# A transformer block forward and backward: one 256 KB load per head in place of four, and fewer DMAs on ScalarE's queue in the backward attention loop

## The chip, the cores and the metric

One core of one Trainium2 chip runs the whole program in one launch. The metric is the device time of an execution in microseconds (us). The engines are PE (matmuls; PEld is its weight load), DVE (VectorE), ACT (ScalarE), POOL (GpSimd) and SP (SyncE, which here only issues DMAs). ACT and POOL can issue DMAs too; an issue stands in the engine's own instruction queue.

## The reference

A block with adaptive layer norm, computed forward and then differentiated. The sequence has S = 2048 tokens of D = 512, 32 heads of 16, and a feed-forward part of width 1792. All arrays are bf16.

```python
mod = silu(c) @ w_mod            # sa, ca, ga, sb, cb, gb: six rows of 512
h = layernorm(x) * (1 + ca) + sa
q, k, v = split(h @ wqkv)        # 32 heads of 16
p = softmax(q @ k.T * 16 ** -0.5)
x = x + ga * ((p @ v) @ wo)
h = layernorm(x) * (1 + cb) + sb
x = x + gb * (relu(h @ w1 + b1) ** 2 @ w2 + b2)
# returned: x, and the gradients of sum(x * grad_out) with respect to
# x, wqkv, wo, w1, b1, w2, b2, c, w_mod
```

## The kernel before

The program has three stretches. The **forward stretch** (to about 1040 us) makes the projections, runs attention by chunks of 512 queries and, a chunk behind, the feed-forward part with its backward pass. It leaves in DRAM what the backward attention needs, feature-major (one row of 2048 tokens for each of the 512 features): `qkT_st` (k and q), `vT_st`, `dOT_st`, and for each head one row of softmax offsets `m_st` and one of sums `d_st`; token-major it leaves `q_st`, `k_st`, `dOs_st`. The **last chunk** (`last_chunk`, to about 1125 us) finishes the dense part and fetches the first head group's rows meanwhile (`head_loads`). The **backward attention loop** (1125 to 2380 us) follows, and then a **tail** with the projections' gradients.

The backward loop treats 8 groups of 4 heads. A head has 16 features, so its rows occupy 16 of 32 partitions, and partition 16 of each 32 holds its `m` or `d` row. The tiles of a group are `k`, `v`, `q`, `do` (128 partitions x 2048 tokens each, profile names `ik`, `iv`, `iq`, `ido`) and `qs` (`iqs`, the group's q token-major). There are two such sets, `hsets[0]` and `hsets[1]`; group hg uses the set hg % 2, and the set of the next group is filled during this one.

A group has 64 units (4 blocks of keys x 16 tiles of queries), four units to a block, so 16 blocks. The order of the instructions on PE, ACT, DVE, SP and POOL is written out by hand: `order_t` and `order_n` are lists of tokens, one list per block in turn, which is why two blocks form the period of the loop. Per unit and head, `score` (L1603) makes a score tile of 128 x 512 on PE, `expo` (L1609) its exponential on ACT; per pair of heads, `dp_pair` (L1623, L1625) makes dP on PE and multiplies by the exponential on DVE into `dS_u`. `k_quad` (L1663) and `v_quad` (L1672) accumulate the gradients of k and v in PSUM (`accVK`).

The gradient of q needs `dS` transposed. `transpose_unit` has SP do this with DMA transposes into `dsT`: two units in one (L1640), and in every second block the third unit alone (L1638); the fourth unit of such a block is transposed on PE (`pe_turn`) and copied by ACT (L1769). Two blocks later `dq_quad` (L1690, `dqacc`) uses `dsT`, and `dq_out` moves the result over ACT (`dqtmp`) and POOL into `dQacc` and `dQst`.

The DMAs beside the transposes are issued on ACT's queue: `at(j, load, to, fro)` puts one behind step j of the loop, where a step is one `D` token (half a unit; 128 to a group), and `load` (L1585) is `ACT.dma_start`. `plan_head(hg)` sets the loads of group hg at every fourth step from step 14 of the group before:

```python
            j0 = (hg - 1) * 128 + 14
            loads = list(kvq_loads(hg)) + list(row_loads(hsets[hg % 2]["do"], dOT_st, hg, slice(0, n), d_st))
            for i, (to, fro) in enumerate(loads):
                at(j0 + 4 * i, load, to, fro)
            at(j0 + 40, spread_qz, hg)
```

`kvq_loads` gives 4 loads of `qs`, then 4 of k, 4 of q with one for the `m` rows, and 4 of v; `row_loads` for dO gives 4 and one for the `d` rows: 22 in all, of 64 KB each but the two for `m` and `d` (16 KB). `spread_qz` copies `qs` into a zero-padded tile on POOL. Each of the four key blocks ends with a store of `vkb` to `dVKtP` (128 KB, groups 0 to 5), and the group with four stores of `dQst` to `dQc` (64 KB each, groups 0 to 6), both on ACT's queue too.

Of the kernel before, what the change touches and what calls it, by code (L numbers as in the profile page):

```python
# [20 lines left out]
P = 128  # L21
# [13 lines left out]
def kernel(  # L35
# [52 lines left out]
    q_st = dram.tile([HG, P, TT, 64], BF, name="q_st")  # L88
    k_st = dram.tile([P, TT, D], BF, name="k_st")
    v_st = dram.tile([n, D], BF, name="v_st")  # L90
    qkT_st = dram.tile([2, D, n], BF, name="qkT_st")
    vT_st = dram.tile([D, n], BF, name="vT_st")
    dOT_st = dram.tile([D, n], BF, name="dOT_st")
    m_st = dram.tile([H, n], BF, name="m_st")
    d_st = dram.tile([H, n], BF, name="d_st")
    wpad_st = dram.tile([D, 8 * P], BF, name="wpad_st")
    wT_st = dram.tile([12, P, D], BF, name="wT_st")
    wmT_st = dram.tile([6, P, 4, D], BF, name="wmT_st")
# [48 lines left out]
    with ExitStack() as ph:  # L147
# [398 lines left out]
        def fload(qc, hg):  # L546
            i = hg % 2
            kt_sb, qt_sb = kts[i], qts[i]
            rows = list(row_loads(kt_sb, qkT_st[1], hg, slice(0, n)))
            rows += row_loads(qt_sb, qkT_st[0], hg, slice(512 * qc, 512 * qc + 512), m_st)  # L550
# [207 lines left out]
        qkT_v = qkT_st.rearrange("a (b p) n -> p a b n", p=P)  # L758
        psp = {}

        def wmod_slice(j):
# [5 lines left out]
        def chunk_cols(g):  # L767
            return slice(512 * g, 512 * g + 512)
# [84 lines left out]
        def prep():  # L853
# [84 lines left out]
            for g in range(QC):  # L938
# [26 lines left out]
                if g == 2:  # L965
                    square(sq[:, 4, :], sP[:, 4, :])
                    norms(4)
            sp(qkT_st[1, 0:P, :], KTs[0][:])
            sp(qkT_st[0, 0:P, 0:512], sP[:, 4, :])
            widest(2)  # L970
            square(sq[:, 3, :], KTs[0][:, chunk_cols(3)])
            norms(3)
# [23 lines left out]
        def plan_tasks():  # L996
# [5 lines left out]
            def key_tile(b, g):  # L1002
                if g == 0:
                    KTs[b] = cb.tile([P, n], BF, name="KT", tag=xtags[b])
                if "k" not in T:
                    T["k"] = cb.tile([P, 4, D], BF, name="sqK", tag="a_c")
                acc = mm()
                turned_proj(acc[:], 1, g, b)
                DVE.tensor_copy(KTs[b][:, chunk_cols(g)], acc[:])
                square(T["k"][:, g, :], KTs[b][:, chunk_cols(g)])  # L1010
                if g == QC - 1:
                    later(1, sp, qkT_st[1, b * P:(b + 1) * P, :], KTs[b][:])

            def key_norm(b, g):
                pn = mm()
# [3 lines left out]
            def query_tile(g, hb):  # L1019
                if "q" not in T:  # L1020
                    T["q"] = cb.tile([P, 4, D], BF, name="sqQ", tag="xn2_c")
                lo = 4 + 4 * (g % 2)
                acc = mm()
                turned_proj(acc[:], 0, g, hb)
                DVE.tensor_copy(sP[:, lo + hb, :], acc[:])
                square(T["q"][:, hb, :], sP[:, lo + hb, :])
                if g == 0:
                    later(1, sp, qkT_st[0, hb * P:(hb + 1) * P, 0:512], sP[:, lo + hb, :])
                elif hb == 3:
                    later(1, sp, qkT_v[:, 0, :, chunk_cols(g)], sP[:, lo:lo + 4, :])  # L1030

            def query_norm(hbs):
                pn = mm()
# [168 lines left out]

        def head_set(i):
            strm.append(tc.alloc_tile_pool(name=f"phIs{i}", bufs=1, side="right"))
            hs = {key: strm[i].tile([P, n], BF, name=f"i{key}{i}") for key in ("k", "v", "q", "do")}
            hs["qs"] = strm[i].tile([P, TT, 64], BF, name=f"iqs{i}")
            hsets.append(hs)

        def head_fill(i):
            for key in ("k", "v", "q", "do"):  # L1210
                POOL.memset(hsets[i][key][:], 1.0 if key in ("k", "v") else 0.0)

        def kvq_loads(hg):
            hs = hsets[hg % 2]
            for i in range(4):
                yield hs["qs"][:, 4 * i:4 * i + 4, :], q_st[hg][:, 4 * i:4 * i + 4, :]
            yield from row_loads(hs["k"], qkT_st[1], hg, slice(0, n))
            yield from row_loads(hs["q"], qkT_st[0], hg, slice(0, n), m_st)
            yield from row_loads(hs["v"], vT_st, hg, slice(0, n))

        def spread_qz(hg):
            to, fro = qz[hg % 2][:, :, :, DH:2 * DH], hsets[hg % 2]["qs"].rearrange("p t (h d) -> p t h d", h=4)
# [19 lines left out]
        def last_chunk(O_c, L, w1T, w2T):  # L1242
# [76 lines left out]
            later(17, copy_const, hsets[0]["v"][:], 1.0)  # L1319
# [182 lines left out]
        with ExitStack() as ph2:  # L1502
            pools["mm"] = ph2.enter_context(tc.tile_pool(name="psM2", bufs=4, space=bass.MemoryType.PSUM))
            with tc.manual_schedule(engines={PE.engine, ACT.engine, DVE.engine, SP.engine, POOL.engine}):
                pools["rs"] = pools["mm"].tile([P, 512], F32, name="rsums", tag="rs", bufs=1)
                DVE.memset(pools["rs"][:], 0.0)
                unit[0] += 1
                run_due()
                L = loads["L"]
                L_dw.append(ffw.tile([P, FC * D], BF, name="dwbuf", tag="wB"))  # L1510
                vaugpool.release()
                head_set(0)
                DVE.memset(hsets[0]["q"][:], 0.0)
                DVE.memset(hsets[0]["do"][:], 0.0)
                copy_const(hsets[0]["k"][:], 1.0)
                O_c = late_finish()
                sp(L["gfT"].rearrange("p t o q -> p (t o) q"), flat(L["gf"]), True)
                for i in range(4):
                    fetch_part(i)
                att.close()  # L1520
                qzpool = tc.alloc_tile_pool(name="qzpool", bufs=1, side="right")
                qz = [qzpool.tile([P, TT, 4, 32], BF, name="qz0")]
                kpool = tc.alloc_tile_pool(name="kpool", bufs=1, side="right")
                dpool = tc.alloc_tile_pool(name="dpool", bufs=1, side="right")
                dwr = tc.alloc_tile_pool(name="dwr", bufs=1, side="right")
                w2T = kpool.tile([P, DC, FF], BF, name="w2T_1", tag="ks")
                for s in range(4):
                    sp(w2T[:, s, :], w2T_st[:, s, :])
                w1T = dpool.tile([P, FC, D], BF, name="w1T_1", tag="dt")
                for s in range(7):  # L1530
                    sp(w1T[:, 2 * s:2 * s + 2, :], w1T_st[:, 2 * s:2 * s + 2, :])

                def head_loads():
                    done = slice(0, 512 * (QC - 1))
                    for i, (to, fro) in enumerate(list(kvq_loads(0)) + list(row_loads(hsets[0]["do"][:, done], dOT_st, 0, done, d_st))):
                        later(i, sp, to, fro)
                    later(12, copy_const, qz[0].rearrange("p t h d -> p (t h d)"), 0.0)
                    later(16, spread_qz, 0)

# [17 lines left out]
    with ExitStack() as ph:  # L1557
# [108 lines left out]
        def v_quad(u):  # L1666
# [57 lines left out]
        for hg in range(1, HG):  # L1724
            plan_head(hg)
        for i, key in enumerate(("q", "k", "v", "do")):
            at((HG - 1) * 128 + 14 + 8 * i, load_grads, "vk", i, hsets[0][key][:])
# [50 lines left out]
    with ExitStack() as ph:  # L1778
# [6 lines left out]
        xs["dq", 1], xs["dq", 2], xs["vk", 4], xs["vk", 5] = (hsets[1][key] for key in ("q", "k", "v", "do"))  # L1785
        xs["dq", 3] = qz[1].rearrange("p t h d -> p (t h d)")
        for key, dsrc, i in (("dq", dQc, 1), ("vk", dVKtP, 4), ("dq", dQc, 2), ("vk", dVKtP, 5)):
            SP.dma_start(out=xs[key, i][:], in_=dsrc[i])
# [271 lines left out]
```

## Time and profile before

| | us |
|---|---|
| runs: median, lowest, highest of 3 | 2517.32, 2511.94, 2524.12 |
| profiled execution, first to last instruction | 2517.6 |
| backward loop within it | 1125 to 2380 |
| one transpose of two units on SP's queue (L1640), median | 5.36 |
| one exponential of 128 x 512 (L1609), from start to start | 0.48 |
| issue of one load on ACT's queue (L1585), median | 0.31 to 0.33 |

The trace's times are of this one profiled execution and count from its first instruction. A row such as `2100.50 0.32 ACTq L1585 DMA_DIRECT2D ik<-qkT_st` gives start, duration, engine, line of the kernel, operation and tiles; `ACTq` and `SPq` are the queues of ACT and SP, where DMA issues stand. Brackets at the end of a row give the engine's idle time ahead of it and what ended it. ACT's exponentials overlap, so a start-to-start distance says more than a duration. A row of windows has the stretch, its length, busy time and count of each engine, the granted TensorE clock (1.00 is full), the share of the DMA engines and GB/s.

### The profile page before, as it was taken

How to read it: one execution, taken by the hardware profiler on the slowest of the kernel's cores; microseconds unless marked ns; L12 is line 12 of the kernel's file. 1: busy time of each engine (PE TensorE's matmuls, PEld its weight loads, DVE VectorE, ACT ScalarE, POOL GpSimd, SP SyncE). 2: the span in 40 equal slices, each digit the busy share in tenths (PEclk: the TensorE clock that was granted, in tenths of full speed). 3: DMA queues.
4: the chain of work that ended last, by engine and by line, in shares of the span. 5: the costliest groups of instructions: out<-in, count | busy, mean ns of one | idle time of the engine just before them, and what ended most of it. 6: DMA issues, size and time to landing. Idle time of an engine off the chain costs nothing. (4 is left out here: it accounts for less than half of the span.)

```text
span 2517.6 us, 49897 instructions
## 1 busy us (share of the span) xinstructions
PE 2342.5 (93%) x19005; PEld 776.3 (31%) x19005; DVE 1810.1 (72%) x2341; ACT 2302.3 (91%) x3577; POOL 350.0 (14%) x379
## 2 busy tenths in 40 slices
PE   7899889989988999999999999999999999999999
PEld 3232223222322323442233322233323323322343
DVE  5556153454435454579999999999999999998862
ACT  7999999999989999539999999999999999999842
POOL 2000000211323142210111101111010111100100
PEclk9999999999999999999999999999999999998999
DMA  6476455367658766979999999999999999999972
GB/s 202 136 193 165 150 122 139 96 161 144 103 85 176 151 134 119 261 208 191 202 199 210 196 206 208 201 207 202 207 202 202 209 195 203 195 208 212 196 237 72
DMA packets 1220981, 447.15 MB, mean 178 GB/s; under 512 B 1096951, under 2 KB 1191607, under 8 KB 1220486
## 3 DMA queue, kind: packets, MB, share of 16 engines
q1 hardware_dynamic: 1192822, 409.11, 82.2%
q0 software_dynamic: 10944, 16.78, 4.8%
q10 hardware_dynamic: 16976, 18.07, 2.8%
q8 instruction: 149, 2.44, 0.4%
q14 instruction: 90, 0.74, 0.1%
HBM read 96.75 MB, written 73.95 MB: 68 GB/s over the span
## 5 line engine op out<-in xcount | busy, mean ns | idle before, releaser
L1625 DVE TENSOR_TENSOR dS_u<-psD_u,E_u 128x1024 bf16<-128x1024 f32 x1024 | 1186.0, 1218 | 71.6 <-PE psD_u L1623 24.0
L567 ACT ACTIVATE ET<-psST 128x1024 bf16<-128x1024 f32 x1024 | 942.0, 1260 | 27.0 <-PE psST L565 26.5
L1609 ACT ACTIVATE E_u<-psS_A 128x512 bf16<-128x512 f32 x768 | 513.1, 668 | 10.5 <-PE psS_C L1603 8.5
L1609 ACT ACTIVATE E_u<-psS_B 128x512 bf16<-128x512 f32 x768 | 505.8, 659 | 12.1 <-DMA dsT<-dS_u 3.0
L1623 PE MATMUL psD_u<-iv,ido 32*128 32x512 bf16 x2048 | 409.6, 388 | 0.0
L565 PE MATMUL psST<-qt_sb,kt_sb 32*128 32x512 bf16 x2048 | 317.8, 387 | 62.0 <-ACT ET L567 46.6
L1609 ACT ACTIVATE E_u<-psS_C 128x512 bf16<-128x512 f32 x512 | 335.4, 655 | 3.3 <-PE psS_B L1603 1.4
L1603 PE MATMUL psS_B<-ik,iq 32*128 32x512 bf16 x768 | 295.3, 385 | 12.8 <-ACT E_u L1609 5.5
L1603 PE MATMUL psS_A<-ik,iq 32*128 32x512 bf16 x768 | 293.4, 382 | 10.9 <-DVE dwlast L237 1.0
L1603 PEld LDWEIGHTS <-iq 32*128 32x128 bf16 x2048 | 130.2, 91 | 316.1 <-issue 298.8
L1663 PE MATMUL accVK<-dS_u,qz 128*32 128x512 bf16 x2048 | 213.3, 390 | 0.4 <-PE psD_u L1623 0.2
L581 PE MATMUL oacc<-ET,vaug 128*32 128x512 bf16 x2048 | 207.7, 396 | 2.2 <-DVE ostage L585 2.2
L1672 PE MATMUL accVK<-E_u,dOs_tok 128*16 128x512 bf16 x2048 | 204.1, 387 | 0.0
L1708 POOL TENSOR_TENSOR dQacc<-dQacc,dqtmp 128x512 f32<-128x512 f32 x64 | 81.2, 1268 | 852.0 <-ACT dqtmp L1703 852.0
L1603 PE MATMUL psS_C<-ik,iq 32*128 32x512 bf16 x512 | 194.7, 380 | 4.2
L565 PEld LDWEIGHTS <-kt_sb 32*128 32x128 bf16 x2048 | 85.8, 91 | 352.2 <-issue 324.6
L1690 PE MATMUL dqacc<-dsT,KS_tok 128*32 128x512 bf16 x2048 | 146.5, 384 | 18.5 <-DMA dsT<-dS_u 4.3
L1769 ACT ACTIVATE dsT<-ptT 128x1024 bf16<-128x1024 bf16 x128 | 145.8, 1139 | 7.9 <-PE ptT L1653 7.3
L251 DVE COPY part<-pm 128x512 f32<-128x512 f32 (+2 forms) x103 | 63.5, 617 | 114.8 <-PE pm L233 111.5
L1623 PEld LDWEIGHTS <-ido 32*128 32x128 bf16 x2048 | 104.6, 91 | 98.9 <-issue 92.9
L1663 PEld LDWEIGHTS <-qz 128*32 128x32 bf16 x2048 | 58.4, 94 | 177.9 <-issue 162.9
L581 PEld LDWEIGHTS <-vaug 128*32 128x32 bf16 x2048 | 53.1, 93 | 121.4 <-issue 121.4
(407 smaller groups left out, 2516.3 us busy)
## 6 DMA issues: line engine op xcount, KB each, us to landing
p_st<-part POOLq DMA_DIRECT2D x36, 256.0 KB, 5.2
kt_sb<-qkT_st SPq DMA_DIRECT2D x124, 64.0 KB
wA<-in_B_w_dram SPq DMA_DIRECT2D x28, 256.0 KB
wB<-w1T_st SPq DMA_DIRECT2D x21, 256.0 KB
wA<-w2T_st SPq DMA_DIRECT2D x21, 256.0 KB
wB<-in_B_w_dram SPq DMA_DIRECT2D x21, 256.0 KB
p_st<-part POOLq DMA_DIRECT2D x25, 192.0 KB, 5.3
p_st<-part SPq DMA_DIRECT2D x18, 256.0 KB
```

The costliest lines, as they stand in the source:

```text
L565: PE.matmul(ps[:, hi, :], kt_sb[r:r + 32, kt * P:(kt + 1) * P], qt_sb[r:r + 32, :], start=True, stop=True, tile_position=(r, 0))
L567: ACT.activation(ET[:, 2 * pair:2 * pair + 2, :], ps[:], AF.Exp, scale=SCALE)
L581: PE.matmul(oacc[32 * hq:32 * hq + 32, :], lhsT, ET[:, hq, :], start=(kt == 0), stop=(kt == TT - 1), tile_position=(0, 32 * hq), skip_grou ...
L1603: PE.matmul(psS[:], st["q"][r:r + 32, qt * P:(qt + 1) * P], st["k"][r:r + 32, kc * 512:kc * 512 + 512], start=True, stop=True, tile_positi ...
L1609: ACT.activation(bst[u][0][:, hq, :], sst.pop((u, hq))[:], AF.Exp, scale=SCALE)
L1623: PE.matmul(psD[:, hi, :], st["do"][r:r + 32, qt * P:(qt + 1) * P], st["v"][r:r + 32, kc * 512:kc * 512 + 512], start=True, stop=True, til ...
L1625: DVE.tensor_tensor(dS_u[:, 2 * pair:2 * pair + 2, :], psD[:], E_u[:, 2 * pair:2 * pair + 2, :], ALU.mult)
L1663: PE.matmul(cur["vk"][32 * hq:32 * hq + 32, :], hst[hg]["qz"][:, qt, hq, :], bst[u][1][:, hq, :], start=(qt == 0), stop=False, tile_positi ...
L1672: PE.matmul(acc[32 * hq:32 * hq + DH, :], dOs_tok[:, qt, (hg * 4 + hq) * DH:(hg * 4 + hq + 1) * DH], E_u[:, hq, :], start=False, stop=(qt ...
L1690: PE.matmul(acc[32 * hq:32 * hq + 32, :], KS_tok[:, kc * 4 + kt, h * DH:h * DH + 32], tT[:, :, hq * 4 + kt, :], start=(kt == 0), stop=(kt ...
L1708: POOL.tensor_tensor(dst2, dst, tmp[:], ALU.add)
L1769: ACT.activation(dst, pt[:], AF.Identity)
```

## The change

The four feature-major arrays become one DRAM tile in which the k, v, q and dO rows of a feature stand side by side, and so do the four tiles of a set in SBUF. One load then brings all four rows of a head's 16 features (16 rows of 16 KB), and one load of 8 KB runs the `m` and `d` rows of the four heads; `qs` comes in one load instead of four. A group has 6 loads, at every 13th step. The stores of `vkb` go two key blocks at a time. In the last chunk the first group's k, v and q come with four loads of 12 KB rows, and dO by itself as before. The places that wrote or read the old arrays use slices of the new ones.

```diff
-    qkT_st = dram.tile([2, D, n], BF, name="qkT_st")
-    vT_st = dram.tile([D, n], BF, name="vT_st")
-    dOT_st = dram.tile([D, n], BF, name="dOT_st")
-    m_st = dram.tile([H, n], BF, name="m_st")
-    d_st = dram.tile([H, n], BF, name="d_st")
+    rows4_st = dram.tile([D, 4, n], BF, name="rows4_st")
+    kT_st, vT_st, qT_st, dOT_st = (rows4_st[:, i, :] for i in range(4))
+    md_st = dram.tile([H, 2, n], BF, name="md_st")
+    m_st, d_st = (md_st[:, i, :] for i in range(2))
...
         def head_set(i):
             strm.append(tc.alloc_tile_pool(name=f"phIs{i}", bufs=1, side="right"))
-            hs = {key: strm[i].tile([P, n], BF, name=f"i{key}{i}") for key in ("k", "v", "q", "do")}
+            rows4 = strm[i].tile([P, 4, n], BF, name=f"irows{i}")
+            hs = {key: rows4[:, j, :] for j, key in enumerate(("k", "v", "q", "do"))}
+            hs["rows"] = rows4
...
-        def kvq_loads(hg):
+        def head_rows(hg, k=4):
             hs = hsets[hg % 2]
-            for i in range(4):
-                yield hs["qs"][:, 4 * i:4 * i + 4, :], q_st[hg][:, 4 * i:4 * i + 4, :]
-            yield from row_loads(hs["k"], qkT_st[1], hg, slice(0, n))
-            yield from row_loads(hs["q"], qkT_st[0], hg, slice(0, n), m_st)
-            yield from row_loads(hs["v"], vT_st, hg, slice(0, n))
+            yield hs["qs"], q_st[hg]
+            for h in range(4):
+                i = (hg * 4 + h) * DH
+                yield hs["rows"][32 * h:32 * h + DH, 0:k, :], rows4_st[i:i + DH, 0:k, :]
+            aux = hs["rows"].rearrange("(h c) a n -> c h a n", h=4)[DH]
+            yield aux[:, 2:k, :], md_st[hg * 4:hg * 4 + 4, 0:k - 2, :]
...
                 def head_loads():
                     done = slice(0, 512 * (QC - 1))
-                    for i, (to, fro) in enumerate(list(kvq_loads(0)) + list(row_loads(hsets[0]["do"][:, done], dOT_st, 0, done, d_st))):
+                    for i, (to, fro) in enumerate(list(head_rows(0, 3)) + list(row_loads(hsets[0]["do"][:, done], dOT_st, 0, done, d_st))):
                         later(i, sp, to, fro)
...
         def plan_head(hg):
             j0 = (hg - 1) * 128 + 14
-            loads = list(kvq_loads(hg)) + list(row_loads(hsets[hg % 2]["do"], dOT_st, hg, slice(0, n), d_st))
-            for i, (to, fro) in enumerate(loads):
-                at(j0 + 4 * i, load, to, fro)
+            for i, (to, fro) in enumerate(head_rows(hg)):
+                at(j0 + 13 * i, load, to, fro)
             at(j0 + 40, spread_qz, hg)
...
                 if hg >= HG - 2:
                     xs["vk", hg] = hst[hg]["vk"]
-                else:
-                    part = slice(kc * 512, (kc + 1) * 512)
+                elif kc % 2 == 1:
+                    part = slice((kc - 1) * 512, (kc + 1) * 512)
                     at(cur["j"] + 4, load, dVKtP[hg][:, part], hst[hg]["vk"][:, part])
```

More of the change, by code (lines that the diff above doesn't have):

```diff
@@ L548, in fload @@
             kt_sb, qt_sb = kts[i], qts[i]
-            rows = list(row_loads(kt_sb, qkT_st[1], hg, slice(0, n)))
-            rows += row_loads(qt_sb, qkT_st[0], hg, slice(512 * qc, 512 * qc + 512), m_st)
+            rows = list(row_loads(kt_sb, kT_st, hg, slice(0, n)))
+            rows += row_loads(qt_sb, qT_st, hg, slice(512 * qc, 512 * qc + 512), m_st)
             for i, (to, fro) in enumerate(rows):
@@ L757 @@
         xtags, htags = ("g_c", "x1_c", "gf", "gfT"), ("T4", "O_c", "h2")
-        qkT_v = qkT_st.rearrange("a (b p) n -> p a b n", p=P)
+        qT_v = qT_st.rearrange("(b p) n -> p b n", p=P)
         psp = {}
@@ L967, in prep @@
                     norms(4)
-            sp(qkT_st[1, 0:P, :], KTs[0][:])
-            sp(qkT_st[0, 0:P, 0:512], sP[:, 4, :])
+            sp(kT_st[0:P, :], KTs[0][:])
+            sp(qT_st[0:P, 0:512], sP[:, 4, :])
             widest(2)
@@ L1011, in key_tile @@
                 if g == QC - 1:
-                    later(1, sp, qkT_st[1, b * P:(b + 1) * P, :], KTs[b][:])
+                    later(1, sp, kT_st[b * P:(b + 1) * P, :], KTs[b][:])
             def key_norm(b, g):
@@ L1027, in query_tile @@
                 if g == 0:
-                    later(1, sp, qkT_st[0, hb * P:(hb + 1) * P, 0:512], sP[:, lo + hb, :])
+                    later(1, sp, qT_st[hb * P:(hb + 1) * P, 0:512], sP[:, lo + hb, :])
                 elif hb == 3:
-                    later(1, sp, qkT_v[:, 0, :, chunk_cols(g)], sP[:, lo:lo + 4, :])
+                    later(1, sp, qT_v[:, :, chunk_cols(g)], sP[:, lo:lo + 4, :])
             def query_norm(hbs):
@@ L1210, in head_fill @@
             for key in ("k", "v", "q", "do"):
-                POOL.memset(hsets[i][key][:], 1.0 if key in ("k", "v") else 0.0)
-        def kvq_loads(hg):
+                POOL.memset(hsets[i][key], 1.0 if key in ("k", "v") else 0.0)
+        def head_rows(hg, k=4):
             hs = hsets[hg % 2]
-            for i in range(4):
-                yield hs["qs"][:, 4 * i:4 * i + 4, :], q_st[hg][:, 4 * i:4 * i + 4, :]
-            yield from row_loads(hs["k"], qkT_st[1], hg, slice(0, n))
-            yield from row_loads(hs["q"], qkT_st[0], hg, slice(0, n), m_st)
-            yield from row_loads(hs["v"], vT_st, hg, slice(0, n))
+            yield hs["qs"], q_st[hg]
[4 more added lines that the diff above has]
+            yield aux[:, 2:k, :], md_st[hg * 4:hg * 4 + 4, 0:k - 2, :]
         def spread_qz(hg):
@@ L1318, in last_chunk @@
             later(8, DVE.memset, dpad[:], 0.0)
-            later(17, copy_const, hsets[0]["v"][:], 1.0)
+            later(17, copy_const, hsets[0]["v"], 1.0)
             rT = cb.tile([P, FC, 512], BF, name="rT", tag="rT")
@@ L1512 @@
                 head_set(0)
-                DVE.memset(hsets[0]["q"][:], 0.0)
-                DVE.memset(hsets[0]["do"][:], 0.0)
-                copy_const(hsets[0]["k"][:], 1.0)
+                DVE.memset(hsets[0]["q"], 0.0)
+                DVE.memset(hsets[0]["do"], 0.0)
+                copy_const(hsets[0]["k"], 1.0)
                 O_c = late_finish()
@@ L1726 @@
         for i, key in enumerate(("q", "k", "v", "do")):
-            at((HG - 1) * 128 + 14 + 8 * i, load_grads, "vk", i, hsets[0][key][:])
+            at((HG - 1) * 128 + 14 + 8 * i, load_grads, "vk", i, hsets[0][key])
         at((HG - 1) * 128 + 46, load_grads, "dq", 0, qz[0].rearrange("p t h d -> p (t h d)"))
@@ L1787 @@
         for key, dsrc, i in (("dq", dQc, 1), ("vk", dVKtP, 4), ("dq", dQc, 2), ("vk", dVKtP, 5)):
-            SP.dma_start(out=xs[key, i][:], in_=dsrc[i])
+            SP.dma_start(out=xs[key, i], in_=dsrc[i])
         SP.dma_start(out=xs["dq", 3][0:64, :], in_=dQc[3, 0:64, :])
```

## The prediction

> **What bounds the kernel now.** I read the head of the page first, then the chain in order of time over the backward loop, then ScalarE's timeline around its DMA issues, then the windows, then the rows of the transposed tile.
>
> ```profile
> PE 2342.5 (93%) x19005; PEld 776.3 (31%) x19005; DVE 1810.1 (72%) x2341; ACT 2302.3 (91%) x3577; POOL 350.0 (14%) x379
> ...
> DMA  6476455367658766979999999999999999999972
> ...
> PE 10%; ACT 8%; DMA 1%; issue 1%; DVE 0%; SPq 0%; ACTq 0%; DVEq 0%
> ```
>
> PE and ACT are both full, and from slice 19 on, the backward loop (1125 to 2380 us), the DMA engines are full too. The chain gives them 1%: a full resource, but seldom the one that ends last. The loop has 128 blocks, and its unit of repetition is a pair of blocks, 8 pairs per head group. The next lines are from the chain in order of time. The first four lie in head group 6, and twelve loads for group 7 are issued between the first and the fourth; the last four are the same places in group 7, which loads nothing from the ACT queue.
>
> ```profile
> 2090.14 1.05 PE dqacc L1690 x16
> ...
> 2109.27 1.05 PE dqacc L1690 x16
> ...
> 2128.57 1.05 PE dqacc L1690 x16
> ...
> 2147.69 1.05 PE dqacc L1690 x15
> ...
> 2247.35 1.05 PE dqacc L1690 x16
> ...
> 2266.47 1.05 PE dqacc L1690 x16
> ...
> 2285.78 1.05 PE dqacc L1690 x16
> ...
> 2304.90 1.05 PE dqacc L1690 x16
> ```
>
> The steps are 19.13, 19.30, 19.12 us with loads and 19.12, 19.31, 19.12 us without. This comparison carries the forecast: the loads that the change merges cost the loop nothing now. Why an issue on ACT costs nothing is in ACT's timeline:
>
> ```profile
> 2100.41 0.60 ACT L1609 ACTIVATE E_u<-psS_C 128x512 bf16<-128x512 f32 x1
> 2100.50 0.32 ACTq L1585 DMA_DIRECT2D ik<-qkT_st  x1
> 2100.88 0.62 ACT L1609 ACTIVATE E_u<-psS_A 128x512 bf16<-128x512 f32 x1
> 2101.36 0.63 ACT L1609 ACTIVATE E_u<-psS_B 128x512 bf16<-128x512 f32 x1
> ```
>
> The exponentials start every 0.48 us with or without the 0.32 us issue between them, because the queue runs ahead of the engine. There is one place where the queue does stop the engine:
>
> ```profile
> 1464.14 0.59 ACT L1609 ACTIVATE E_u<-psS_A 128x512 bf16<-128x512 f32 x1
> 1467.36 0.34 ACTq L1585 DMA_DIRECT2D dQc<-dQst  x1
> 1467.76 0.60 ACT L1609 ACTIVATE E_u<-psS_B 128x512 bf16<-128x512 f32 x1 [3.03 <-DMA dsT<-dS_u]
> ```
>
> Here the last of four `dQc` stores stands in ACT's queue and waits for a transpose that has nothing to do with its data. In the trace the DMAs of SP and ACT take one of eight completion semaphores in turn, and an issue waits until the previous user of its semaphore has landed; that was the transpose into `dsT` whose issue ended at 1464.37. The pair in the windows (length; ACT busy; clock), with the same pair of the next group under it:
>
> ```profile
> 1457.00:1480.20 23.20, 19.12 (x37) 0.93 1.20 218
> 1613.30:1633.00 19.70, 19.12 (x38) 1.00 1.17 216
> ```
>
> 3.5 us: 3.03 of idle ACT, the rest a drop of the granted clock right behind it (half clock from 1469.9 to 1473.3).
>
> **The change part by part.** The span is 2517.6 us, the median of the runs 2517.3, so a sum made on the span holds for the runs. PE and DVE keep their order in the built program; ACT issues 116 DMAs where it issued 240, SP 834 where it issued 845.
>
> *Issues taken from ACT.* Per group, 22 loads become 6, and 4 `dVKtP` stores become 2 (where there are stores): 7 x 16 + 12 = 124 issues less, at 0.31 to 0.34 us (0.50 for the small rows) some 40 us of queue time. The cover is the exponential that the engine is still working on (0.48 us for 0.32 us). By the comparison above I take 0. Were the cover gone, the gain would be those 40 us. [...]
>
> *The stall at 1464 us.* In the trace the fourth `dQc` store is issued 1.9 to 2.5 us after the transpose that it depends on has landed in five groups, and in group 2 the landing comes 1.2 us too late by the packets, more with the signal. In the changed program fewer DMAs stand between two users of a semaphore: the same store depends on a transpose one older, with 3.8 us in hand in that group and 6.9 to 7.8 in the others. So this stall goes, -3.5 us. Behind it nothing is late: the pair is then 19.7 us like its neighbours. The neighbours' own 0.4 to 0.6 us over 19.18 stay, for group 7, which has no loads, shows 0.57 there too.
>
> *What is added: one load moves 256 KB.* 16 rows of 16 KB, one for each DMA engine, 28 such loads in the loop beside the transposes. Bounds: a 4 KB packet takes 159 ns, so a row is at least 4 x 159 = 0.64 us; the sixteen packets of one 64 KB load spread over 0.51 us, so four times that, 2.0 us. A merged load holds the engines for 0.6 to 2.0 us in one go, where four loads did it in parts of 0.16 to 0.5. Who sees it: the transposes, and behind them `dqacc` on PE, two blocks later:
>
> ```profile
> L1640 SPq DMA_TRANSPOSE dsT<-dS_u x192: 4769/5364/6827, 1133.2 to 2378.8; - x192
> ...
>   DMA dsT<-dS_u: 4.3, 2
> ```
>
> First is the transpose's issue (min, median, max in ns; the spread is what other traffic adds), then, from the tile's rows, what PE waited for it: 4.3 us in 2 of 128 blocks. From the last packet to `dqacc` there are mostly 4 to 7 us, and never under 1.5 in the groups that load. A fit over the 192 issues gives 0.14 us more for each 64 KB load beside one, and 0.33 for each 16 KB instruction-fetch packet, the row nearest to the new one. Four merged loads at 0.33 to 0.6 are 1.3 to 2.4 us per group against 16 x 0.14 = 2.2 now. I take 0 for the loop; without the slack it would be 28 x 0.6 to 2.0 = 18 to 56 us.
>
> *Edits with one answer.* The `q_st` load in one piece (2 KB runs for 512 B), stores of two `vk` parts in one, later loads (the last one 65 steps after the first, where it was 84): 0; all arrive dozens of microseconds before the next group begins. In the last chunk SP issues 11 DMAs less at 0.32 to 0.4 us, 4 us; PE is busy for 20.00 of 20.00 us there (1060 to 1080), so 0. The forward part keeps its order and its waits. Its rows in DRAM now lie 16 KB apart in place of 4 KB; no row prices that, its loads are 4 KB runs as before and stand a group ahead, so 0, with 2 us either way.
>
> *Where the clock drops.* Eight pairs of the loop are longer than their kind; five by 1.3 us, each with one 3.4 us window at half clock though PE was busy for 95 to 97% before it. [...] Any shift redraws them: 0, with 4 us either way.
>
> Sum: 2517.3 - 3.5 = 2513.8, taken as 2514.
>
> **The rivals.**
> *Nothing to be seen.* The stall at 1464 was this execution's; others have it elsewhere or not (the runs spread over 12 us), and the clock windows hide the rest: 2517.
>
> *Faster: traffic and issues do cost.* From group 1 on, the loop's pairs exceed their clean length (19.34 and 19.18 us in turn) by 18.7 us in all. If nearly all of that came from ACT's queue being held, from transposes made late by the many small DMAs, and from the clock drops that follow, it would be 2517 - 17 = 2500. It takes two thirds of the 18.7 to pass 0.5%. For it: ten `dQc` issues take 0.97 to 1.84 us where 0.31 is usual, most of them right behind another issue. Against it: group 7, without loads, has the longest of them, and 7.2 of the 18.7.
>
> *Slower: the large load makes the transposes the bound.* The issues of the transposes fill 146 to 153 us of a group's 154.5; the gaps in SP's queue sum to 3.5 to 8.9 us per group in groups 1 to 6, 6.4 on average. If one merged load adds d, a group needs 4d - 2.2 more of it. It decides from d = 2.2 us; at 3 us it is 4 x 3 - 2.2 - 6.4 = 3.4 us per group, 24 us with 7 groups: 2541. At the bound from rows, 2.0, it stays hidden. [...]
>
> *Slower: more clock drops.* Twelve in place of five, 9 us: 2523.
>
> **How the numbers follow.** The forecast has 0.50, nothing 0.24, more clock drops 0.05; all three lie within 0.5% (12.6 us, about what a measurement of this kernel can tell from no change): 0.79. Faster by traffic and issues 0.13, slower by the large load 0.08. The range takes the forecast with 4 us of clock and 2 us of DRAM either way, reaches down towards the faster rival and up to the drops and the first microseconds of the slower one: 2502 to 2526; that leaves out about 1 in 10 to 2 in 10.
>
> **What would show it.** Right: the steps between `dqacc` lines stay at 19.12 to 19.34 us in all groups; no ACT idle time that ends on `dsT<-dS_u`; ACT's issue rows show 116 DMAs. Wrong on the merged load: L1640's median rises from 5.36 us, SP's gaps vanish, `dqacc` waits for `dsT` in many blocks. Wrong on the issues: steps under 19.1 us, or the pair with the four `dQc` stores down to 19.2.

## The result, and the profile after

| | before | after |
|---|---|---|
| median of 4 runs, us | 2517.79 | 2556.86 |
| lowest, highest | 2511.94, 2524.12 | 2548.88, 2562.00 |
| profiled span | 2517.6 | 2555.6 |
| its backward loop | 1254.5 | 1288.8 |

The ratio is 1.014, 95% interval 1.011 to 1.017: slower by some 35 us by the ratio and 39 by the medians, where 2514 was forecast and the range ended at 2526. The two profiled spans differ by 38.0 us: 34.3 in the loop, 4.7 ahead of it, -1.0 behind it.

From the head of the page and its chain of work:

```profile
PE 2362.3 (92%) x19005; PEld 778.5 (30%) x19005; DVE 1813.0 (71%) x2341; ACT 2305.9 (90%) x3577; POOL 350.4 (14%) x379
...
PE 40%; ACT 34%; DMA 8%; issue 8%; DVE 7%; SPq 2%; POOL 0%; ACTq 0%; DVEq 0%; POOLq 0%
```

ACT does the same work (2305.9 us for 2302.3); PE's 20 us more go with the clock (92.2 us of the loop at half in place of 44.4, below). The chain now has 8% of DMA. The 1% before the change is no measure for it: that chain could be followed back only to about 1995 us, and its shares sum to 20%. Run 3 below leaves the row loads out and is as fast as the kernel before; its chain reaches back nearly to the start and has 4%:

```profile
PE 41%; ACT 37%; issue 8%; DVE 7%; DMA 4%; SPq 1%; POOL 0%; ACTq 0%; DVEq 0%; another core or an unknown queue 0%; POOLq 0%
```

The chain after the change in order of time through head group 6, the one whose even steps carried the forecast (start, duration, what):

```profile
2126.88 1.05 PE dqacc L1691 x16
...
2166.46 7.77 DMA dsT<-dS_u
...
2177.60 11.18 DMA dsT<-dS_u
2188.91 1.05 PE dqacc L1691 x16
...
2210.35 1.05 PE dqacc L1691 x16
...
2229.53 1.05 PE dqacc L1691 x16
...
2248.87 1.05 PE dqacc L1691 x16
```

Two transposes stand in the chain ahead of a `dqacc`; two loads of 256 KB were issued at 2166.25 and 2181.64. The next step is 21.44 us; once the loads are over the steps are 19.18 and 19.34 again. The transposed tile's rows, the issue (min/median/max) and what PE waited for it:

```profile
L1641 SPq DMA_TRANSPOSE dsT<-dS_u x192: 4797/5213/10734, 1138.1 to 2418.0; - x192
...
  DMA dsT<-dS_u: 19.0, 14
...
  DVE dS_u L1626: 9.9, 7
```

The maximum rises from 6.8 to 10.7 us and the waits from 2 to 14. The median falls from 5.36 to 5.21, for most transposes now have no load beside them: the harm is in the tail. The last row, DVE among those that waited for the transposes, is a second way from a late transpose to PE, which the prediction did not name. The tile `dS_u` has four buffers, and DVE cannot fill the next one before a transpose has read it. DVE waited 9.9 us for that, where it did not wait at all before, and PE waited in turn for DVE (us in total, times, longest):

```profile
PE psD_u L1624 <- DVE dS_u L1626: 5.4, 6, 1.7
```

What one load does, in the windows before, during and after the first one of the loop (after the busy times: clock, DMA share, GB/s):

```profile
1163.00:1167.80 4.80, 4.57 (x48) 1.26 (x48) 4.80 (x5) 4.76 (x11) 0.00 (x0) 1.00 1.09 195
1167.80:1174.80 7.00, 6.88 (x66) 2.22 (x59) 6.89 (x7) 7.00 (x14) 0.00 (x0) 1.00 1.24 71
1174.80:1177.00 2.20, 2.19 (x19) 0.86 (x18) 2.06 (x3) 2.20 (x5) 0.00 (x0) 1.00 1.36 241
```

While the load is in flight, the engines are as full as ever by their packets' time (share 1.24) and move 71 GB/s where they moved 195: the packets are under way, but take longer. The chain at the same place shows what follows from it, with ACT's issue of the load from the timeline in a fence of its own:

```profile
1164.76 14.89 DMA dsT<-dS_u
...
1179.79 1.07 PE dqacc L1691 x16
```

```profile
1165.59 0.33 ACTq L1587 DMA_DIRECT2D irows<-rows_st  x1
```

The loop's 34.3 us have three parts. PE waits 14.7 us more for `dsT` (19.0 for 4.3) and 5.4 us for `dS_u`. The clock is at half for 92.2 us of the loop in place of 44.4; at the 1.3 us that a 3.4 us window cost before, an estimate of 47.8 / 3.4 x 1.3 = 18 us. Together that is 38 us, somewhat more than was measured. That these windows follow the waits is not proved by one trace, but it goes with them through the runs below: 27 to 55 us of half clock in the eight kernels of the table that lose at most 16 us by the median, 61 to 171 us in the change and the ten others, which lose 25 us or more.

### The profile page after: what moved, and what is told of

It reads as the page before. It is cut to its first block, busy times and chain, and to the rows that moved or that the text cites. A ratio compares the mean times of both kernels' runs of the same rounds, so it can differ in the third digit from the quotient of the medians.

```text
span 2555.6 us, 49719 instructions
## 1 busy us (share of the span) xinstructions
PE 2362.3 (92%) x19005; PEld 778.5 (30%) x19005; DVE 1813.0 (71%) x2341; ACT 2305.9 (90%) x3577; POOL 350.4 (14%) x379
## 4 chain that ended last, share of the span: by engine, by line
PE 40%; ACT 34%; DMA 8%; issue 8%; DVE 7%; SPq 2%; POOL 0%; ACTq 0%; DVEq 0%; POOLq 0%
ACT E_u L1610 21%; ACT ET L566 9%; DMA dsT<-dS_u 5%; PE psST L564 4%; PE dqacc L1691 4%; PE pm L232 3%; PE psS_A L1604 2%; SPq L177 2%; PE oacc L580 2%; ACT dsT L1770 2%; PE accVK L1664 2%; PE psS_B L1604 2%; PE pdh L1885 2%; PE pm L413 2%; PE pwq L1919 2%
## 5 line engine op out<-in xcount | busy, mean ns | idle before, releaser
L1610 ACT ACTIVATE E_u<-psS_A 128x512 bf16<-128x512 f32 x768 | 505.3, 658 | 17.3 <-DMA out_dram<-xlast 7.2
L1610 ACT ACTIVATE E_u<-psS_B 128x512 bf16<-128x512 f32 x768 | 499.8, 651 | 20.5 <-PE psD_u L1624 15.7
L1624 PE MATMUL psD_u<-irows 32*128 32x512 bf16 x2048 | 412.4, 392 | 5.6 <-DVE dS_u L1626 5.4
L1604 PE MATMUL psS_A<-irows 32*128 32x512 bf16 x768 | 297.6, 387 | 10.4 <-DVE dwlast L236 0.9
L1604 PE MATMUL psS_B<-irows 32*128 32x512 bf16 x768 | 299.0, 389 | 8.0 <-ACT E_u L1610 0.5
L1604 PEld LDWEIGHTS <-irows 32*128 32x128 bf16 x2048 | 129.9, 91 | 319.0 <-issue 302.0
L1604 PE MATMUL psS_C<-irows 32*128 32x512 bf16 x512 | 195.0, 381 | 4.7 <-ACT dqtmp L1704 0.2
L1624 PEld LDWEIGHTS <-irows 32*128 32x128 bf16 x2048 | 105.0, 91 | 103.1 <-issue 97.4
L1654 PE MATMUL ptT<-identb,dS_u 128*128 128x128 bf16 x1024 | 84.7, 230 | 6.9 <-DVE dS_u L1626 0.4
```

The source lines that it names most:

```text
L1604: PE.matmul(psS[:], st["q"][r:r + 32, qt * P:(qt + 1) * P], st["k"][r:r + 32, kc * 512:kc * 512 + 512], start=True, stop=True, tile_positi ...
L1610: ACT.activation(bst[u][0][:, hq, :], sst.pop((u, hq))[:], AF.Exp, scale=SCALE)
L1624: PE.matmul(psD[:, hi, :], st["do"][r:r + 32, qt * P:(qt + 1) * P], st["v"][r:r + 32, kc * 512:kc * 512 + 512], start=True, stop=True, til ...
L1654: PE.transpose(pt[:, i, :], held["dS"][:, 2 * half + i // 4, kt * P:(kt + 1) * P], identb[:])
```

## The experiments

The runs in one table. "SP more" is what the SP issues of the transposes of groups 0 to 6 take beyond the run without row loads (1017.0 us), for each row load; "waits" is PE's idle time until `dsT`, without the way over `dS_u`, and "half" the loop's time at half clock. All three are in us and from one profiled execution, which in runs 2, 6, 7, 8 and 13 was the fastest of its kernel. Medians are of 4 to 12 executions, and each ratio is against executions of the kernel before that were taken beside them.

```
run                          row loads a group   median  ratio (95%)              SP more  waits  half
before                       16 x 64 KB          2517.8                            0.25      4.3    44
after                        4 x 256 KB          2556.9  1.0140 (1.0110-1.0170)    2.50     19.0    92
1  per array                 16 x 64             2524.0  1.0027 (1.0010-1.0043)    0.25      4.6    44
2  pieces of 4 KB            4 x 256             2546.8  1.0119 (1.0078-1.0160)    2.39     11.7    61
3  no rows                   -                   2521.4  1.0007 (0.9987-1.0026)    -         4.7    55
4  twice                     8 x 256             2609.9  1.0351 (1.0313-1.0389)    2.40     45.2   154
5  per array, old layout     16 x 64             2521.0  1.0014 (0.9998-1.0030)    0.27      4.7    27
6  halves                    8 x 128             2533.6  1.0071 (1.0043-1.0099)    0.87      8.3    34
7  four adjacent rows        16 x 64             2638.1  1.0482 (1.0457-1.0507)    1.46     54.0   171
8  as 5, small gradients     16 x 64             2532.4  1.0053 (1.0033-1.0072)    0.27      5.5    31
9  far partitions            4 x 256             2532.9  1.0058 (1.0029-1.0087)    1.85      9.2    48
10 four in a burst           16 x 64             2598.3  1.0320 (1.0273-1.0368)    0.18      5.6   147
11 one of four merged        1 x 256, 12 x 64    2523.3  1.0029 (1.0009-1.0049)     -        8.3    41
12 one row of sixteen        4 x 16              2515.9  1.0003 (0.9987-1.0018)    0.15      5.0    34
13 shifted by 8              4 x 256             2557.2  1.0175 (1.0125-1.0226)    2.47     15.6    75
14 one row of each head      16 x 64             2560.5  1.0170 (1.0145-1.0195)    0.82     21.6    79
15 24 steps apart            4 x 256             2559.6  1.0173 (1.0146-1.0201)    2.19      4.8    92
16 the same, behind stores   4 x 256             2545.1  1.0119 (1.0092-1.0145)    2.56     18.3    65
17 stores apart too          4 x 256             2556.9  1.0135 (1.0098-1.0173)    3.16     31.9    68
18 as 16, two steps on       4 x 256             2569.3  1.0193 (1.0163-1.0224)    3.53     15.3    89
```

**Is it the merged loads?** Runs 1, 3 and 4. Run 1, in `plan_head` (run 3 issues only `qs` and `aux`):

```diff
-            for i, (to, fro) in enumerate(head_rows(hg)):
-                at(j0 + 13 * i, load, to, fro)
+            qs, *rows, aux = head_rows(hg)
+            at(j0, load, *qs)
+            for i in range(16):
+                to, fro = rows[i % 4]
+                at(j0 + 4 + 4 * i, load, to[:, i // 4, :], fro[:, i // 4, :])
+            at(j0 + 68, load, *aux)
```

> The changed kernel with the four rows of a head loaded again by one DMA for each array (16 loads of 64 KB per head group, each a quarter of what one merged load moves), still out of the DRAM tile with rows 16 KB apart; the merged q_st load, the merged md load and the merged dVKtP stores stay. Theory A (the 256 KB that one load moves in one go keep the transposes waiting, their SP issues grow from 5.0 to 6-10 us, dqacc waits, and the clock drops behind each stall): back to 2517, within 6 us, the transposes' 2-unit issues at most 7 us. Theory B (the DRAM layout, or the other merges, cost the time): stays at 2550 to 2560.

> The changed kernel without the row loads of head groups 1 to 7 (the q_st and md loads stay; later groups compute on old rows, so this part of the computation is left out). It bounds what these loads cost in all. Theory A: 2510 to 2517, that is, all of the 39 us and at most some us of what the loads cost before the change. Theory B: stays near 2555.

Run 4 keeps the change and adds, at `j0 + 13 * i + 6`, each row load once more.

> The changed kernel with every merged row load of the loop issued twice, the second six steps after the first (the same data into the same place). Theory A: the price per load again, 28 more loads at 1.4 us (39 / 28): 2585 to 2610, more if the second finds the queue of the transposes already late. Theory B: within 5 us of the changed kernel, 2557.

All three go theory A's way, though run 1 ends 1 us and run 3 4 us above the range that was expected. Cut into four, the loads cost hardly anything; without them the kernel is where it was before, so 16 loads of 64 KB are as good as free. Twenty-eight more merged loads cost 53 us, more each than the first 28 (1.9 us to 1.3). The loss is the merged loads'.

**Is it the layout in DRAM, or the forward part?** Run 5 is run 1 with

```diff
-    rows4_st = dram.tile([D, 4, n], BF, name="rows4_st")
+    rows4_st = dram.tile([4, D, n], BF, name="rows4_st")
```

> The changed kernel with one 64 KB load for each array again and with the DRAM tile as [4, D, n] (rows of one array one behind the other): of the change only the merged q_st and md loads and the merged dVKtP stores are left. Theory A (what is left of the loss in the run with loads for each array, 1.0027, is the forward part's rows lying 16 KB apart): the loop begins at 1125 us again in place of 1130, and the time is 2514 to 2520. Theory B (the few merged small transfers cost it): 2524 as in that run, with the loop beginning at 1125. Theory P (the prediction without its merged load): 2514.

It is 2521.0, and its interval overlaps run 1's; no cost of the layout is shown. Its loop began at 1133.0 us with the old layout, run 6's at 1124.0 with the new one: over all these profiles the loop begins between 1123.4 and 1134.1 in either layout. So the 4.7 us ahead of the loop lie within that scatter.

**Piece length, bytes, or engines held?** Run 2 has the old layout with one load for a head (64 pieces of 4 KB), run 6 two loads of 128 KB for a head, run 7 four loads of four whole rows (`to[4 * r:4 * r + 4]`), run 12 only the first of the 16 rows (`to[0:1]`).

> The changed kernel with the DRAM tile as [4, D, n] in place of [D, 4, n]: one load per head as before, 256 KB, 12 DMAs per head group, but in 64 pieces of 4 KB in place of 16 of 16 KB. Theory A1 (it is the long piece: a DMA engine that has begun 16 KB lets no transpose packet in for 1.5 us and more): back to about 2520. Theory A2 (it is the 256 KB in one go, whatever the pieces): stays at 2545 to 2560. Theory B (the layout in DRAM): 2517 as well, so it is told from A1 by the run with one load for each array.

> The changed kernel with each merged load cut into two of 128 KB (two arrays each, pieces of 8 KB), 8 row loads per head group in place of 4. Theory A with a price that follows the bytes that one DMA moves in one go and the slack of 4 to 7 us: nearly back, 2520 to 2530, hardly a transpose issue over 7 us. If the price were per byte of merged rows: it stays at 2550 to 2557.

> The changed kernel with each merged load cut by rows: four loads of 4 rows of 16 KB (64 KB each), so the long pieces stay and the 256 KB in one go do not. Theory A1 (the long piece of 16 KB counts): 2540 to 2557. Theory A2 (the bytes in one go count): 2520 to 2526 as with one load for each array.

> The changed kernel with each merged load cut to one of its 16 rows (16 KB on one DMA engine, 28 of them; the other rows are not loaded, so later groups compute on old rows). Theory A with the price of the 16 KB instruction fetch (0.33 us of transpose issue, one engine): 2519 to 2525, 0.3 to 0.6 us per load; the prediction then took its price from a row of one engine for a load of sixteen. Rival (one held engine stops a transpose as well as sixteen): 2540 and more, 2 us per load.

Pieces of 4 KB leave most of the cost: the long piece is not the cause. Half the bytes cost a third (0.87), with a time 4 us above what was expected. But run 7 overturned the theory of bytes in one go: its loads are 64 KB like run 1's, and it is the slowest kernel of all, slower than either theory allowed. Its row of the transposes, and run 12's:

```profile
L1646 SPq DMA_TRANSPOSE dsT<-dS_u x192: 4814/5606/9597, 1137.7 to 2495.8; - x192
```

```profile
L1644 SPq DMA_TRANSPOSE dsT<-dS_u x192: 4759/4998/6962, 1135.6 to 2375.5; - x192
```

One row of 16 KB costs nothing that the times show (0.15 us of issue, less than was expected), four of them at neighbouring partitions do.

**Neighbouring partitions.** Run 9 writes a head's 16 rows 8 partitions apart, run 13 is its control, with equally misplaced rows at 16 adjacent partitions; run 14 is run 7 with one row of each head, 32 partitions apart, in place of four adjacent rows.

```diff
+            far = hsets[hg % 2]["rows"].rearrange("(c h) a n -> h c a n", h=8)
+                at(j0 + 13 * (i + 1), load, far[2 * i], fro)                     # run 9
...
+                at(j0 + 13 * (i + 1), load, hsets[hg % 2]["rows"][32 * i + 8:32 * i + 24], fro)   # run 13
...
+            to = hsets[hg % 2]["rows"].rearrange("(h c) a n -> c h a n", h=4)    # run 14
+            fro = rows4_st.rearrange("(g h c) a n -> g c h a n", h=4, c=DH)[hg]
+            for c in range(DH):
+                at(j0 + 4 + 4 * c, load, to[c], fro[c])
```

> The changed kernel, its 28 merged loads (256 KB, 16 rows of 16 KB) with the 16 rows written 8 partitions apart over the whole tile in place of 16 adjacent partitions (so the heads are computed on wrongly placed rows). Theory A (each of 16 DMA engines is held by its 16 KB, wherever the rows go): as the changed kernel, 2550 to 2560, 2.2 to 2.7 us more of transpose issue per load. [...]

> The control for the run with rows 8 partitions apart: the merged loads write 16 adjacent partitions as in the changed kernel, but 8 partitions further on (so the heads are computed on wrongly placed rows, as there). Rival P (the nearness of the partitions counts, not the data): 2548 to 2562. If the odd data made that run fast: 2525 to 2540.

> Sixteen loads of 64 KB per head group, each four rows of 16 KB as in the run that took 2638 us, but one row of each of the four heads, 32 partitions apart, in place of four adjacent rows; the data are the right ones. Rival P: far below 2638, at 2521 to 2545, and 0.25 to 0.7 us of transpose issue per load where the four adjacent rows had 1.46. Theory A (an engine held by 16 KB is what counts, four of them in both): 2620 to 2650.

Rival P, by which the nearness of the partitions counts, holds in direction: with the same bytes and the same 256 KB, far partitions lose 15 us where near ones lose 40 (run 13, so it is not the data); with the same four rows of 16 KB, run 14 loses 43 us where run 7 loses 120. It does not hold in full: both runs end above what was expected with it (at most 2530 and 2545), and run 9 still has 1.85 us for each load where the change has 2.50. So the bytes of a load count beside the nearness of its partitions.

The traces show how long the transposes are kept out. Their packets of 256 bytes in each half microsecond, from half a microsecond before a load's first packet, mean over a kernel's loads:

```
5  64 KB, 16 rows of 4 KB            432 | 251 288 309 395 389 431 439
12 16 KB, 1 row                      388 | 272 193 355 348 432 428 422
14 64 KB, 4 far rows of 16 KB        468 | 292 122  95 232 345 379 392
9  256 KB, 16 far rows               355 |  88  42 156 242 257 281 314
after  256 KB, 16 adjacent rows      335 | 102  13  39 116 162 160 253
2  256 KB, 64 pieces of 4 KB         368 | 105  18  33 112 171 165 298
6  128 KB, 16 rows of 8 KB           448 | 144 175 177 263 328 349 375
7  64 KB, 4 adjacent rows of 16 KB   521 | 364  53  77  73  63 184 439
```

The transposes' packets stay under 170 for 0, 0, 1.0 and 1.5 us in runs 5, 12, 14 and 9, for 3.0 us after the change and for 2.0 us in run 7, and the single row's packet took 0.61 us. Run 2 goes as the change does, whatever the length of its pieces.

With equal bytes the nearer partitions keep the transposes out twice as long: 64 KB for 2.0 us at four adjacent partitions (run 7) and 1.0 us at partitions 32 apart (run 14), 256 KB for 3.0 us at 16 adjacent ones (the change) and 1.5 us at 16 that are 8 apart (run 9). The limit of 170 was chosen after the fact; at 150 the change and run 9 are at 2.0 and 1.0 us. Run 6 fits less well: with half the bytes of the change at the same partitions, half of 3.0 would be an estimate of 1.5 us, and the trace has 0.5. What it is in near partitions that does this, no run shows.

**Is the slack of 4 to 7 us of use?** Run 11 merges only the first head's load; run 15 keeps all four, 24 steps apart (`j0 + 4 + 24 * i`).

> Per head group the first head's rows by a merged load of 256 KB, the other three heads' by loads of 64 KB: 7 merged loads in place of 28. Theory A with the same price each: 2521 + 7 x 1.3 = 2530. If the slack of 4 to 7 us covers a single one with room around it, and only the next one while the transposes are still late costs time: 2521 to 2524.

> The changed kernel with its merged loads 24 steps (three blocks) apart in place of 13. If a load costs time only where the transposes are still late from the one before: 2520 to 2535. If each has its own price of 1.3 us: 2550 to 2560.

Run 11 is at 2523.3, but its interval (2520 to 2530) takes in both values. Run 15 is as slow as the change, which speaks for a price of each load; its trace says otherwise. All but 12 of its 64 pairs of blocks are within 1 us of their clean length, those with the last three loads of a group nearly all; the loss lies in the second pair of groups 1 to 6 (24.6 to 30.6 us for 19.1), where its first load stands in ACT's queue just ahead of the four `dQc` stores. ACT's timeline there:

```profile
1315.95 0.60 ACT L1613 ACTIVATE E_u<-psS_A 128x512 bf16<-128x512 f32 x1
1323.60 0.32 ACTq L1587 DMA_DIRECT2D dQc<-dQst  x1
1323.96 0.60 ACT L1613 ACTIVATE E_u<-psS_B 128x512 bf16<-128x512 f32 x1 [7.41 <-DMA dsT<-dS_u]
```

That is the stall that the prediction read at 1464 us, now in six groups, 29.4 us in all. Run 16 moves the loads behind the stores (`j0 + 18 + 24 * i`), run 17 also takes the stores three steps apart (`cur["j"] + 6 + 3 * hq`).

> The changed kernel with its merged loads 24 steps apart, the first at step 32 of the group in place of 27, behind the four dQc stores (steps 18 to 21). If a merged load three blocks from the next is covered by the slack, and the loss of the run before was the stores' wait for a semaphore: 2515 to 2525, all pairs of blocks near their clean length. If each merged load has a price of its own: 2545 to 2560.

> As the run with the merged loads 24 steps apart and behind the stores, and the four dQc stores of a group three steps apart in place of one. If the stores' semaphore wait is what is left in that pair: 2 to 6 us below that run. If it is not: within 2 us of it.

Run 16's expectation failed: 2545. The stall is gone, but `dqacc` waits for `dsT` 13 times, in pairs that were clean in run 15. Run 17 came out as neither of its two expectations said: 2556.9, over a spread from 2536 to 2565. The next idea was the place in the block; run 18 is run 16 two steps on (`j0 + 20 + 24 * i`).

> The merged loads 24 steps apart as in the run before, each two steps later (steps 34, 58, 82, 106 of the group: step 2 of a block in place of step 0). If the place in the block decides (in the run that began at step 18 the 21 loads at step 2 behind the stores left their pairs clean): 2517 to 2527. If each merged load has its price wherever it stands: 2540 to 2550 as before.

2569, above both expectations: the step doesn't decide it. In its trace the way over `dS_u` is the larger one, which the column "waits" leaves out: PE waits 19.1 us for DVE there, for 2.3 in run 16. What the traces show afterwards, over the 168 merged loads of the change and runs 13 and 15 to 18: where a load's first packet comes 0.5 to 2.5 us after a transpose's issue began (134 loads), this transpose and the next take 2.3 us more on average; in the other 34, very early or later in the issue, 5.0 us. The two kinds overlap: single loads reach 8.9 us in the first and 7.1 in the second, and run 18 has 22 of its 28 loads in the first and is the slowest of the four. A step of the order does not hold this place, since the transposes' issues shift against the blocks. No run varied it alone, so it is a reading, not a test, and whether a merged load can be hidden in the slack stays open.

**Two side runs.** Run 10, with the old layout, issues a head's four 64 KB loads in one step; run 8 cuts the five gradient loads of 512 KB in group 7 into 40 of 64 KB on ACT's queue.

> One 64 KB load for each array, but the four of a head issued one behind the other in the same step where the merged load stood: the same bytes at the same places, four DMAs. Theory A, the merging itself counts (a DMA's pieces stand in one row at an engine, and four DMAs let transposes in between): 2520 to 2530, 0.25 to 0.5 us of transpose issue per load. Theory A', only the bytes in so short a time count: 2540 to 2557, 2 us and more for each four loads.

> As the run with loads for each array and the DRAM tile as [4, D, n], and beside it the five loads of gradients in head group 7 (512 KB each on SP's queue, between the transposes) cut into 40 loads of 64 KB on ACT's queue, which has no loads in that group. Theory A (what counts is the bytes that one DMA moves beside the transposes): group 7 falls from 160 to about 155 us and the time by 3 to 6 us below that run, 2509 to 2514. Rival (forty more issues on ACT cost as much, or the loads cost nothing): no change or slower.

Run 10's loss is a third mechanism: its transposes are hardly longer (0.18 us per load), but the loads hold ACT's queue:

```profile
1183.03 2.82 ACTq L1587 DMA_DIRECT2D irows<-rows_st  x3
1185.95 0.60 ACT L1614 ACTIVATE E_u<-psS_C 128x512 bf16<-128x512 f32 x1 [2.26 <-DVE dS_u L1630]
```

Three issues take 2.82 us where one alone takes 0.31, and the next exponential comes 2.3 us late; PE waits 55 us for `E_u` in the loop. What holds the issues was not tested. Run 8 is 11 us slower than run 5, against the theory. Its profiled execution was its fastest (2517.3) and shows only group 7 at 162.1 us for 158.8; where the rest goes stays open. No version beat the kernel before: with no row load at all it is no faster.

## Why the prediction was wrong, point by point

*The DMA engines' 1% of the chain:* misread. The chain covered only the last 520 us of the program (its shares sum to 20%), so it could not show that DMA seldom ends last in the rest. In runs 1 and 3, which are about as fast, DMA has 4%. The conclusion drawn beside it, that the 64 KB loads cost nothing, rests on the equal steps and is borne out by run 3.

*Issues taken from ACT, at 0:* right. Run 3 issues none of the row loads and stands at 1.0007 (0.9987 to 1.0026); the rival in which traffic and issues cost is out. The cover has a limit that the prediction did not see: run 10, where four loads come one right behind another, loses 80 us.

*The stall at 1464 us, -3.5:* half right. In the changed kernel the fourth store's issue no longer stops the exponentials:

```profile
1485.91 0.62 ACT L1610 ACTIVATE E_u<-psS_C 128x512 bf16<-128x512 f32 x1
1486.49 0.60 ACT L1610 ACTIVATE E_u<-psS_A 128x512 bf16<-128x512 f32 x1
1486.50 0.51 ACTq L1587 DMA_DIRECT2D dQc<-dQst  x1
1487.06 0.60 ACT L1610 ACTIVATE E_u<-psS_B 128x512 bf16<-128x512 f32 x1
```

But run 5, which is the change without the merged row loads, is not faster than before (1.0014, lower end 0.9998; -3.5 us would be 0.9986): its profile has 4.2 us of the same wait in three other places. The dependence on the semaphore's last user moved with the DMAs that were added or taken, in run 5 to those three places, in run 15 into six groups (29.4 us); it was booked as a gain for good.

*What is added, at 0 for the loop:* this is the step that failed, twice. First the size: it took 0.33 to 0.6 us of transpose issue per load from the 16 KB instruction fetch, with 2.0 us as the upper bound. It is 2.50 (run 4: 2.40). The row was that of a single 16 KB packet (a single row, run 12, costs 0.15 us); sixteen rows at 16 adjacent partitions are another thing. The rival with the large load, at a chance of 0.08, had its turning point at 2.2 us and its sum at 3 us, and the measured 2.50 lies between them. Second the cover: the slack ahead of `dqacc` was taken to hide a mean. In the traces the two transposes at a load took from 0.5 to 8.9 us more, and SP has 3.6 to 10.5 us of gaps in a whole group to win that back, so that the next load can meet transposes that are still late. And `dqacc` is not alone in waiting: late transposes also hold the buffers of `dS_u` (9.9 us of DVE, 5.4 of PE), a way for which the prediction had no term.

*The rival with the large load* had the mechanism and not the size. With the measured 2.5 us its own sum gives 4 x 2.5 - 2.2 - 6.4 = 1.4 us per group, 2527 in all. It let the gaps of a whole group pay for the loads; in the trace gaps remain, 3.6 us in the fullest group that loads, and `dqacc` has waited all the same. And it had no term for the clock, by the estimate above about half of the loss.

*Edits with one answer; forward, 2 us either way:* no cost of theirs is shown; the bound was too narrow, as the start of the loop scatters over 11 us. *Where the clock drops, 4 us either way:* wrong, an estimated 18 us. That a shift only redraws the drops was the author's estimate and no run shows it; in the runs the half clock goes with the loss, 27 to 55 us of it in the kernels that lose at most 16 us and 61 to 171 us in those that lose 25 us or more. Of the signs named, the median of L1641 was a bad one (it fell), SP's gaps did not vanish, and `dqacc`'s waits came as described, if in 14 of 128 blocks.

## What to carry to other kernels

Beside a stream that is nearly full and that PE waits for, price a load by the longest time for which it keeps that stream out. Here that time went with the bytes of one load (at 16 adjacent partitions 0, 0.5 and 3.0 us under 170 packets for 64, 128 and 256 KB) and with how near their partitions lie (2.0 us for 1.0, 3.0 for 1.5). The loss went hardly with the number of loads (16 of 64 KB a group 1.0014 in run 5, none 1.0007 in run 3), as long as these did not stand one right behind another (run 10, 1.0320). Merging 64 KB loads whose issues are hidden anyway had nothing to win here, and putting four rows side by side turned four short stops (251 packets in the lowest half microsecond of run 5) into a long one (13 after the change). Compare the largest single delay, at the worst place, with the slack, never the mean of a group with the sum of its gaps. Follow a late transfer to everything that waits for it, its reader and the buffers that it holds; and price the half clock that came with the waits (an estimated 18 us of the loss here) beside the waits themselves.

## What was not expected of the hardware

Four rows of 16 KB at adjacent partitions stop the transposes for some 2 us, four at partitions 32 apart for 1 us (2638 and 2560 us for the kernel), though both loads are 64 KB in four pieces. The share of the DMA engines does not show it: 1.24 at 71 GB/s, 1.09 at 195. And while the loads' packets in the change took 1.45 us each (median), a row alone took 0.61.
